# Sixteen blocks of w3 fetched in the last steps of the first network, into the tiles that later hold the product

## The chip, the cores and the metric

The kernel runs on one core of one Trainium2 chip, as one launch. The metric is the time of an execution on the device in microseconds; the time of a kernel is the median of its runs.

## The reference, cut to what matters

Three layers follow one another, all in fp32:

```
attn: state = gamma*state + k v^T; y = scale * q state      # 4 batches, 8 heads, 768 steps, head size 64
x  = attn as [3072, 512]
h  = x @ w_in [512, 2048];  g = min(max(h,1), clipped square of (h+1)/2)
x  = g @ w_out [2048, 512]                                  # first network
a  = x @ w1 [512, 1024];  b = x @ w2 [512, 1024]
h  = (a*b) @ w3 [1024, 1024]
out = h @ w_out2 [1024, 512]                                # second network
```

Nothing lies between the product with w3 and the one with w_out2, so the kernel multiplies w3 by w_out2 first (1024 x 512) and uses that product instead of both.

## The kernel before, in words

The order of the instructions is written by hand: each engine runs its own list in the order of the program, and waits only for data and for buffers. SP issues nearly all DMAs, in order; POOL issues the stores of prepared weights.

**First network.** The tokens lie in six tiles of 512. A step n multiplies one tile by one 128-wide column of w_in (`emit_h`) and adds the result of step n-1, times a row block of w_out, to the accumulators (`emit_y1`). A step holds 24 matmuls of 128 x 512. Every fp32 factor is split into a high and a low part in fp32r (`split`, L97 to L99: ScalarE copies the high part, VectorE subtracts it), and three matmuls stand for one product (`mm3`: high x high, low x high, high x low; L102 to L104). So a matmul on L102 needs the high part alone, the next one on L103 the low part.

**The last 16 steps (f = 0 to 15).** While the last tile runs, the weights of the second network, which earlier steps have converted and stored in DRAM (`spill`), come back. `fetch` issues a load on SP into one of two rings of tiles in the pool `late`: tag "f" with two buffers for blocks of w_out2 and w3, tag "y" with four buffers for blocks of w1 and w2 ("wab") and later for the first network's result. Even f: load_wo2(j - 1) splits a block of w_out2, a fetch takes the next one, and `fetch_ab(j + 1)` takes a pair of w1/w2 blocks. Odd f up to 11: `prepare_ab(j)` turns pair j into seven sums and copies (it is a Strassen-like scheme), splits them into the two stage tiles "four" and "three", and POOL stores these to DRAM (`wab_d`, 1024 and 768 KB). Before a stage tile is written again, its store has to have landed.

**The product w3 x w_out2 (u = 0 to 15).** In it a block of w3 (128 x 512, 256 KB) is split by `load_w3(u)` into one of two "ws" tiles; the split for u + 1 stands ahead of the matmuls of u, so it needs the tile that u - 1 has read. `emit_w3o(u)` is 12 matmuls into four PSUM banks. After u = 7 and u = 15 `evac_w3o` splits the four banks into tiles of tag "wc" (eight tiles of 128 x 2 x 512), which hold the product to the end. Other work is laid between: `prepare_ab(6)` at u = 0, `fetch_ab(7)` behind it, `prepare_ab(7)` at u = 3 and behind it four loads of the first network's result (`fetch_y1(0, 0)`) into the "y" buffers that the preparation frees; `add_y(0, 0)` at u = 5 adds them (VectorE, L650 to L653; the second operation, L651, needs the last of the four loads); splits (`split_y`) at u = 5 to 15; `fetch_y1(0, 1)` at u = 7 and `add_y(0, 1)` at u = 8 do the same for the other half; `load_unit` at u = 11 and 13 loads prepared weights.

**The second network** (`emit_ab`, matmuls on L673; `emit_out`, L718 to L720) follows, with TensorE nearly always busy.

Lines that the change and the prediction touch: L273 (which ring a fetch takes), L275 (the DMA of `fetch`), L559 to L563 (`load_w3`), L577 to L581 (`evac_w3o`), L842 to L858 (the fetches of the last steps), L866 to L870 (the loop over u).

Of the kernel before, what the change touches and what calls it, by code (L numbers as in the profile page):

```python
# [9 lines left out]
F32 = mybir.dt.float32  # L10
# [6 lines left out]
P = 128  # L17
# [9 lines left out]
NF1, NF2 = FF1 // P, FF2 // P  # L27
# [22 lines left out]
def retention_then_two_ffns(  # L50
# [17 lines left out]
    nc = tc.nc  # L68
# [26 lines left out]
    late = None  # L95

    def split(hi, lo, src):  # L97
        nc.scalar.copy(out=hi, in_=src)  # L98
        nc.vector.tensor_tensor(out=lo, in0=src, in1=hi, op=ALU.subtract)  # L99
# [9 lines left out]
    spill = {}  # L109
# [5 lines left out]
    def load_job(j):  # L115
        src, n, key, _ = j
        if key not in loaded:
            loaded.add(key)
            raw = cpool.tile([P, 2 * n], U32, tag="raw", name="raw")
            if key[0] == "win":  # L120

                to = raw.rearrange("p (f h a w) -> p f h a w", h=2, a=2, w=2 * P)
                of = src.bitcast(U32).rearrange("p (f a c w) -> p f a c w", a=2, c=2, w=2 * P)
                for h in range(2):
                    for c in range(2):
                        for i in range(n // 512):
                            nc.sync.dma_start(
                                out=to[64 * c:64 * c + 64, i, h], in_=of[64 * h:64 * h + 64, i, :, c]
                            )
            else:  # L130
                nc.sync.dma_start(out=raw, in_=src.bitcast(U32))
            raws[key] = raw
            ready[("raw", key)] = dma(n, max(now["dve"], now["pe"] - 4.0))

    def new_w(name):
        return wpool.tile([P, 2, 512], F32R, tag="w", name=name)
# [103 lines left out]
    def done_spill(key):  # L240
        def done(w, u):
            nc.vector.tensor_tensor(out=w, in0=w, in1=u, op=ALU.add)
            d = dram.tile([P, 512], F32, name=f"sp_{key[0]}_{key[1]}")
            nc.sync.dma_start(out=d, in_=w)
            spill[key] = d
            yield 0.73

        return done
# [16 lines left out]
    def drain_conv():  # L265
        while jobs or conv is not None:
            run_conv(1)


    arrived = {}  # L270

    def fetch(key, src):
        one = key[0] in ("wo2", "w3")  # L273
        t = late.tile([P, 512], F32, tag="f" if one else "y", name="f32", bufs=2 if one else 4)
        nc.sync.dma_start(out=t, in_=src)  # L275
        arrived[key] = t
# [221 lines left out]
    def fetch_part(i):  # L498
        y1_st[i] = []
        for m in range(NK):  # L500
            st = work.tile([P, TT], F32, tag="st", name="y1st", bufs=4)
            nc.sync.dma_start(out=st, in_=y1_part[i][m])
            y1_st[i].append(st)
# [45 lines left out]
    wo2 = {}  # L549
    w3 = {}  # L550
    wc = {}
    accs = {}

    def load_wo2(j):
        t = new_w("wo2")
        split(t[:, 0, :], t[:, 1, :], arrived.pop(("wo2", j)))
        wo2[j] = t

    def load_w3(u):  # L559
        if u < 2 * NF2:  # L560
            t = split_pool.tile([P, 2, 512], F32R, tag="ws", name="w3s")
            split(t[:, 0, :], t[:, 1, :], arrived.pop(("w3", u)))
            w3[u] = t  # L563
# [40 lines left out]
    def fetch_ab(f):  # L604
        for w in range(2):
            fetch(("wab", 2 * f + w), spill[("wab", 2 * f + w)])
# [128 lines left out]
    with tc.manual_schedule():  # L735
# [6 lines left out]
        for at_, (kind, w, f, done) in enumerate(order):  # L742
# [3 lines left out]
            for i in range(2):  # L746
                one = (w[f // 2][:, i * 512:(i + 1) * 512], 512, (kind, f + i), done(f + i))
# [28 lines left out]
        for n in range(-1, NA):  # L776
            last = n + 1 == NA
            if n < HALF - 1:
                mine = 1 if n % 2 else 2
            elif n < NF1 + 3:  # L780
                mine = 0
            elif n < NF1 + HALF - 2:
                mine = 1
            elif n < 2 * NF1 - 1:
                mine = (len(todo) - (NSTEP - 3 * TILE_PIECES) + 2 * NF1 - 2 - n) // (2 * NF1 - 1 - n)
            else:
                mine = 1 if (n + 1) % 4 < 3 else 0
            mine = [todo.popleft() for _ in range(mine) if todo]
            if n == PLAIN - 1:
                drain_conv()  # L790
                conversion.close()
                split_pool = splits.enter_context(tc.tile_pool(name="split_pool", bufs=2))
                cpool = conversion.enter_context(tc.tile_pool(name="cpool1", bufs=2))
                jobs.extend(later)
                load_job(jobs[0])
                load_job(jobs[1])
                for j in range(NF2):
                    jobs.append((w_out2[j], 512, ("wo2", j), done_spill(("wo2", j))))
                for j in range(NF2):
                    for i, w in enumerate((w1, w2)):  # L800
                        key = ("wab", 2 * j + i)
                        jobs.append((w[j], 512, key, done_spill(key)))
                for u in range(2 * NF2):
                    hf, j = divmod(u, NF2)
                    key = ("w3", u)
                    jobs.append((w3t[j][:, hf * 512:(hf + 1) * 512], 512, key, done_spill(key)))
            for i in range(2):
                if n == NF1 + (i + 1) * HALF - 4:
                    fetch_part(i)
            if n == NA - NF1:  # L810
                assert not todo
                drain_conv()
            f = n - (NA - NF1)
            if not last:
                emit_h(n + 1)
            if mine:
                piece_mm(mine[0])
                chunk_ahead(mine[0])
            if not last:
                emit_g1(n + 1)  # L820
            if mine:
                piece_ew(mine[0])
            if not last and f:
                emit_g2(n + 1)
            if n >= 0:
                emit_y1(n)
                evac_y1(n)
            if not f:

                conversion.close()  # L830
                splits.close()
                retention.close()
                split_pool = ctx.enter_context(tc.tile_pool(name="split_late", bufs=2))
                late = ctx.enter_context(tc.tile_pool(name="late", bufs=1))
                emit_g2(n + 1)
            if not last:
                emit_wo(n + 1)
            for a in mine[1:]:
                piece_mm(a)
                chunk_ahead(a)  # L840
                piece_ew(a)
            if f >= 0:  # L842
                if f % 2 and f < 2 * EARLY_AB:
                    prepare_ab(f // 2)
                elif f % 2 == 0:
                    j = f // 2
                    if j == 0:
                        fetch_ab(0)
                    else:
                        load_wo2(j - 1)  # L850
                    fetch(("wo2", j), spill[("wo2", j)])
                    if 0 <= j < EARLY_AB:
                        fetch_ab(j + 1)
                    if j == NF2 - 1:
                        fetch(("w3", 0), spill[("w3", 0)])
                elif last:
                    load_wo2(NF2 - 1)
                    fetch(("w3", 1), spill[("w3", 1)])  # L858
        pairs_psum.close()
        ps_b = ctx.enter_context(tc.tile_pool(name="ps_b", bufs=1, space=bass.MemoryType.PSUM))  # L860

# [4 lines left out]
        load_w3(0)  # L866
        for u in range(2 * NF2):
            load_w3(u + 1)
            if u + 2 < 2 * NF2:
                fetch(("w3", u + 2), spill[("w3", u + 2)])  # L870
            emit_w3o(u)
            hf, j = divmod(u, NF2)
            if j == NF2 - 1:
                evac_w3o(hf)
            if u == 0:
                prepare_ab(EARLY_AB)
                fetch_ab(EARLY_AB + 1)
            elif u == 3:
                prepare_ab(EARLY_AB + 1)
                fetch_y1(0, 0, range(4))  # L880
            elif u == 5:
                add_y(0, 0)
            elif u == 7:
                fetch_y1(0, 1, range(4))
            if u == 5:
                split_y(*ahead.pop(0))
            elif u in (6, 7, NF2):
                split_y(*ahead.pop(0))
                split_y(*ahead.pop(0))
            elif u > NF2:  # L890
                split_y(*ahead.pop(0))
            if u == NF2:
                add_y(0, 1)
            if u in (2 * NF2 - 5, 2 * NF2 - 3):
                load_unit((u - 2 * NF2 + 5) // 2)
# [104 lines left out]
```

## Time and profile before

| | |
|---|---|
| median of 3 runs | 1108.78 us (1108.28 to 1109.03) |
| the profiled execution | 1105.77 us, its span 1104.0 us |
| mean granted TensorE clock | 0.985 |
| PE busy | 1050.3 us, 95% of the span, 5444 matmuls |
| DVE, ACT, POOL busy | 698.7, 433.9, 71.5 us |
| DMA queue of SP and the like (q1) | 150.44 MB, 40.1% of 16 engines |
| DMA queue of POOL (q0) | 14.68 MB, 3.7% of 16 engines |
| chain that ended last | PE 84%, DVE 6%, DMA 5%; the loads `f<-sp_w` alone 2% |

PE is TensorE, PEld its weight loads, DVE VectorE, ACT ScalarE, SPq the instruction queue of SP. `f<-sp_w` is a load of a block of w3 from DRAM into a tile of tag "f", `f<-y_d` one of the first network's result into a tile of tag "y", `w3s` the split block, `wc` the finished product. A matmul's busy time overlaps the next one's, so the distance between two starts tells the pace, not the duration. "granted clock" 1.00 stands for 2.4 GHz and 0.50 for 1.2 GHz.

### The profile page before, as it was taken

Reading aid. Unit: us, or ns where it says so; the run is one execution under the profiler, and the core shown is the slowest. Engines: PE = TensorE matmul, PEld = TensorE weight load, DVE = VectorE, ACT = ScalarE, POOL = GpSimd, SP = SyncE. Lnnn points to the kernel's source line nnn. Section 1 sums busy time; section 2 is a strip of 40 time slices with the busy share of each in tenths; the row PEclk is TensorE's granted clock in tenths of the full one; section 3 lists DMA queues with packets and bytes.
Section 4 is the critical chain, followed back from the end, with each engine's and each line's share of the span. In section 5 each row is a group of like instructions: output and inputs, shape, how many; then the busy total and the mean of one; then the engine's idle time right before and its main releaser. Section 6 shows DMA issues by size and latency. Waiting matters only on the chain.

```text
span 1104.0 us, 14147 instructions
## 1 busy us (share of the span) xinstructions
PE 1050.3 (95%) x5444; PEld 828.7 (75%) x5444; DVE 698.7 (63%) x1130; ACT 433.9 (39%) x763; POOL 71.5 (6%) x67
## 2 busy tenths in 40 slices
PE   4789999899999999999999998689999999999998
PEld 3555578677777777777788886478888888888886
DVE  4798888688888878877835774553445334623340
ACT  1223355344444445454435664432333223412220
POOL 2212000011110100000000010000000000000000
PEclk9789999999999999999999999899999999999999
DMA  6545225254443544354303665554544345523412
GB/s 208 181 154 181 77 96 183 85 172 173 164 152 124 170 136 153 124 173 142 115 2 132 248 239 196 185 200 172 187 166 143 131 176 172 189 105 134 167 34 77
DMA packets 64116, 166.03 MB, mean 150 GB/s; under 512 B 7600, under 2 KB 15920, under 8 KB 59312
## 3 DMA queue, kind: packets, MB, share of 16 engines
q1 hardware_dynamic: 61744, 150.44, 40.1%
q0 software_dynamic: 2304, 14.68, 3.7%
q8 instruction: 43, 0.70, 0.2%
q14 instruction: 25, 0.20, 0.1%
HBM read 125.24 MB, written 39.85 MB: 150 GB/s over the span
## 4 chain that ended last, share of the span: by engine, by line
PE 84%; DVE 6%; DMA 5%; ACT 2%; SPq 1%; issue 1%; POOL 1%; ACTq 0%; POOLq 0%; DVEq 0%
PE bank_a L673 12%; PE hps L103 8%; PE y1acc L102 8%; PE hps L102 8%; PE hps L104 8%; PE y1acc L103 7%; PE y1acc L104 7%; PE bank_b L673 6%; PE oacc L718 4%; PE oacc L720 4%; PE oacc L719 4%; PE bank_c L673 3%; PE pa L372 3%; DMA f<-sp_w 2%; PE y1acc L513 2%; PE pa L348 2%
## 5 line engine op out<-in xcount | busy, mean ns | idle before, releaser
L102 PE MATMUL hps<-xh,win 128*128 128x512 f32 x384 | 154.7, 403 | 6.3 <-ACT win L98 5.0
L103 PE MATMUL hps<-xh,win 128*128 128x512 f32 x384 | 151.7, 395 | 0.5 <-DVE win L99 0.5
L104 PE MATMUL hps<-xl,win 128*128 128x512 f32 x384 | 150.8, 393 | 0.4 <-DVE xl L417 0.4
L673 PE MATMUL bank_a<-yop,unit 128*128 128x512 f32 x576 | 145.7, 389 | 0.0
L102 PE MATMUL y1acc<-gh,wo_s 128*128 128x512 f32 x340 | 139.0, 409 | 4.9 <-ACT wo_s L98 4.9
L461 ACT ACTIVATE r<-hps 128x512 f32<-128x512 f32 x96 | 57.3, 597 | 218.3 <-PE hps L104 218.3
L103 PE MATMUL y1acc<-gh,wo_s 128*128 128x512 f32 x340 | 134.2, 395 | 0.5 <-DVE wo_s L99 0.5
L104 PE MATMUL y1acc<-gl,wo_s 128*128 128x512 f32 x340 | 133.6, 393 | 0.0
L463 DVE SCALAR_TENSOR_TENSOR r<-hps,r 128x512 f32<-128x512 f32 x96 | 66.3, 691 | 101.2 <-ACT r L462 100.7
L673 PEld LDWEIGHTS bank_a<-yop,unit 128*128 128x128 f32 x576 | 108.1, 188 | 22.5
L699 DVE TENSOR_TENSOR c<-bank_b,c 128x512 f32<-128x512 f32 x24 | 16.6, 692 | 131.5 <-PE bank_b L673 131.5
L102 PEld LDWEIGHTS hps<-xh,win 128*128 128x128 f32 x384 | 72.6, 189 | 25.2 <-ACT win L98 5.7
L103 PEld LDWEIGHTS hps<-xh,win 128*128 128x128 f32 x384 | 72.6, 189 | 18.6 <-DVE win L99 1.6
L104 PEld LDWEIGHTS hps<-xl,win 128*128 128x128 f32 x384 | 72.7, 189 | 17.0 <-DVE xl L417 1.3
L102 PEld LDWEIGHTS y1acc<-gh,wo_s 128*128 128x128 f32 x340 | 64.1, 189 | 23.7 <-ACT wo_s L98 5.7
L104 PEld LDWEIGHTS y1acc<-gl,wo_s 128*128 128x128 f32 x340 | 64.1, 189 | 14.5
L103 PEld LDWEIGHTS y1acc<-gh,wo_s 128*128 128x128 f32 x340 | 64.2, 189 | 13.9 <-DVE wo_s L99 1.6
L474 ACT CAST gh<-r 128x512 fp32r<-128x512 f32 x85 | 52.9, 622 | 52.6 <-DVE r L463 52.6
L673 PE MATMUL bank_b<-yop,unit 128*128 128x512 f32 x288 | 73.1, 389 | 0.0
L475 DVE TENSOR_TENSOR gl<-r,gh 128x512 fp32r<-128x512 f32 x85 | 60.6, 713 | 14.9 <-ACT gh L474 13.8
L99 DVE TENSOR_TENSOR wo_s<-wo_f,wo_s 128x512 fp32r<-128x512 f32 x85 | 61.9, 728 | 1.9 <-ACT wo_s L98 1.9
L315 POOL TENSOR_TENSOR q_t<-q_t,decay 128x512 f32<-128x512 f32 x23 | 32.6, 1416 | 465.4 <-DMA q_t<-in_qT_dram 438.0
(152 smaller groups left out, 1716.6 us busy)
## 6 DMA issues: line engine op xcount, KB each, us to landing
unit<-wab_d SPq DMA_DIRECT2D x24, 1024.0 KB, 4.8
unit<-wab_d SPq DMA_DIRECT2D x24, 768.0 KB, 4.3
raw<-in_w_in_dram SPq DMA_DIRECT2D x64, 128.0 KB, 3.0
raw<-in_w_dram SPq DMA_DIRECT2D x16, 512.0 KB, 4.0
raw<-in_w3t_dram SPq DMA_DIRECT2D x16, 512.0 KB, 3.8
wab_d<-four POOLq DMA_DIRECT2D x8, 1024.0 KB, 5.2
raw<-in_w_out_dram SPq DMA_DIRECT2D x14, 512.0 KB, 3.6
q_t<-in_qT_dram SPq DMA_DIRECT2D x24, 256.0 KB, 4.4
```

Source lines behind the costliest of these rows:

```text
L99: nc.vector.tensor_tensor(out=lo, in0=src, in1=hi, op=ALU.subtract)
L102: nc.tensor.matmul(out=ps, lhsT=lh, rhs=rh, start=first, stop=False)
L103: nc.tensor.matmul(out=ps, lhsT=ll, rhs=rh, start=False, stop=False)
L104: nc.tensor.matmul(out=ps, lhsT=lh, rhs=rl, start=False, stop=last)
L461: nc.scalar.activation(out=r, in_=hps[n], func=AF.Relu, bias=0.5, scale=0.5)
L463: nc.vector.scalar_tensor_tensor(out=r, in0=hps.pop(n), scalar=1.0, in1=r, op0=ALU.max, op1=ALU.min)
L474: nc.scalar.copy(out=gh, in_=gs[n])
L475: nc.vector.tensor_tensor(out=gl, in0=gs[n], in1=gh, op=ALU.subtract)
L673: nc.tensor.matmul(out=ps, lhsT=x, rhs=z, start=first and kb + k == 0, stop=kb == 1 and k == 2, skip_group_check=True,)
L718: nc.tensor.matmul(out=ps, lhsT=lh, rhs=wh, start=(f == 0), stop=False)
L719: nc.tensor.matmul(out=ps, lhsT=lh, rhs=wl, start=False, stop=False)
L720: nc.tensor.matmul(out=ps, lhsT=ll, rhs=wh, start=False, stop=(f == NF2 - 1))
```

## The change

`fetch` keeps tag "f" for blocks of w_out2 alone. A new `fetch_w3(u)` takes one tile of tag "wc" and loads two blocks of w3 into its two halves. It is called once in each of the steps f = 8 to 15, at the step's end, and so all 16 blocks are issued by the end of the first network, into all eight "wc" tiles. The fetches of w3 at f = 14, at f = 15 and in the loop over u go. `load_w3` and everything else stay as they are; `evac_w3o` takes its "wc" tiles from the same eight.

```
 def fetch(key, src):
-    one = key[0] in ("wo2", "w3")
+    one = key[0] == "wo2"
     t = late.tile([P, 512], F32, tag="f" if one else "y", name="f32", bufs=2 if one else 4)
     nc.sync.dma_start(out=t, in_=src)
     arrived[key] = t
...
+def fetch_w3(u):
+
+    t = late.tile([P, 2, 512], F32, tag="wc", name="w3f", bufs=NF2)
+    for i in range(2):
+        nc.sync.dma_start(out=t[:, i, :], in_=spill[("w3", u + i)])
+        arrived[("w3", u + i)] = t[:, i, :]
...
                 fetch(("wo2", j), spill[("wo2", j)])
                 if 0 <= j < EARLY_AB:
                     fetch_ab(j + 1)
-                if j == NF2 - 1:
-                    fetch(("w3", 0), spill[("w3", 0)])
             elif last:
                 load_wo2(NF2 - 1)
-                fetch(("w3", 1), spill[("w3", 1)])
+            if f >= NF2:
+                fetch_w3(2 * (f - NF2))
...
     for u in range(2 * NF2):
         load_w3(u + 1)
-        if u + 2 < 2 * NF2:
-            fetch(("w3", u + 2), spill[("w3", u + 2)])
         emit_w3o(u)
```

## Rows read from the trace of the kernel before

**Rows 1.** Busy by stretch: PE, PEld, DVE, ACT, POOL; granted clock, DMA share, GB/s.
```profile
640.00:650.00 10.00, 10.00 (x46) 8.27 (x45) 7.47 (x17) 6.97 (x16) 1.06 (x2) 1.00 0.61 232
676.00:689.00 13.00, 12.16 (x44) 9.39 (x45) 6.48 (x16) 4.01 (x10) 1.06 (x2) 0.87 0.77 258
...
700.00:712.00 12.00, 7.07 (x17) 5.28 (x18) 6.15 (x10) 3.57 (x7) 0.00 (x0) 0.72 0.54 194
712.00:723.00 11.00, 8.11 (x34) 5.81 (x32) 9.11 (x16) 6.73 (x13) 0.00 (x0) 1.00 0.36 124
```
**Rows 2.** Waits from 676 to 741 us: total, times, longest.
```profile
ACT w3s L98 <- DMA f<-sp_w: 21.2, 4, 8.4
```
**Rows 3.** Chain that ended last, in order of time: start us, us, what.
```profile
696.48 0.32 SPq L275
696.85 7.31 DMA f<-sp_w
704.26 0.63 ACT w3s L98
...
717.66 2.62 DMA f<-y_d
```
**Rows 4.** PE in order of time: start us, us, operation; in brackets idle before, releaser.
```profile
679.47 0.63 PE L104 MATMUL w3acc<-wo,w3s 128*128 128x512 f32 x1
...
680.97 0.39 PE L102 MATMUL w3acc<-wo,w3s 128*128 128x512 f32 x1
...
704.93 0.80 PE L102 MATMUL w3acc<-wo,w3s 128*128 128x512 f32 x1 [5.04 <-ACT w3s L98]
...
721.73 0.49 PE L102 MATMUL w3acc<-wo,w3s 128*128 128x512 f32 x1 [1.85 <-ACT w3s L98]
...
723.05 0.50 PE L103 MATMUL w3acc<-wo,w3s 128*128 128x512 f32 x1 [0.83 <-DVE w3s L99]
...
725.45 0.39 PE L104 MATMUL w3acc<-wo,w3s 128*128 128x512 f32 x1
...
739.70 1.52 PE L673 MATMUL bank_a<-yop,unit 128*128 128x512 f32 x6
```
**Rows 5.** VectorE in order of time, 676 to 713 us.
```profile
676.03 0.69 DVE L99 TENSOR_TENSOR w3s<-f,w3s 128x512 fp32r<-128x512 f32 x1
...
692.55 0.42 DVE L619 TENSOR_TENSOR s<-f 128x256 f32<-128x256 f32 x1
...
696.37 0.68 DVE L99 TENSOR_TENSOR w3s<-f,w3s 128x512 fp32r<-128x512 f32 x1
...
706.12 0.68 DVE L651 TENSOR_TENSOR t__5952<-f,f 128x512 f32<-128x512 f32 x1
...
708.65 0.68 DVE L99 TENSOR_TENSOR w3s<-f,w3s 128x512 fp32r<-128x512 f32 x1
...
712.46 2.77 DVE L99 TENSOR_TENSOR wc<-w3acc,wc 128x512 fp32r<-128x512 f32 x4 [0.32 <-ACT wc L98]
```
**Rows 6.** ScalarE in order of time: a stage tile's split, a split of w3.
```profile
656.72 0.71 ACT L98 CAST three<-s 128x256 fp32r<-128x256 f32 x2
...
725.88 0.62 ACT L98 CAST w3s<-f 128x512 fp32r<-128x512 f32 x1 [2.63 <-PE w3acc L104]
```
**Rows 7.** POOL in order of time: the second store of pair 4.
```profile
648.29 0.53 POOL L627 DMA_DIRECT2D wab_d<-three  x1 [0.47 <-DVE three L99]
```
**Rows 8.** DMAs issued at 648.29, 694.80, 696.48 and 696.75 us: KB, us to landing.
```profile
wab_d<-three POOLq DMA_DIRECT2D x1, 768.0 KB, 6.9
...
f<-y_d SPq DMA_DIRECT2D x1, 256.0 KB, 2.5
...
f<-y_d SPq DMA_DIRECT2D x1, 256.0 KB, 5.0
...
wab_d<-three POOLq DMA_DIRECT2D x1, 768.0 KB, 7.2
```
**Rows 9.** SP's queue in order of time: the loads of pair 5.
```profile
635.47 2.00 SPq L275 DMA_DIRECT2D f<-sp_wab  x2
```

## Prediction

> **What bounds the kernel now.** The page gives TensorE 95% of the span, so the missing 5% are sought first. The view of busy time by stretch shows where part of them lies: in the last steps of the first network TensorE is busy without a break, but in the product w3 x w_out2 it lacks 0.84 of 13 us, 4.93 of 12 and 2.89 of 11, and in two of these stretches the granted clock is down as well, to 0.87 and 0.72 on average [rows 1]. In full-speed work that is another 13 x 0.13 = 1.7 us and 12 x 0.28 = 3.4 us. The view of waits names what ended last: ScalarE's splits of w3 wait 21.2 us in four waits for the load of their block [rows 2]. The chain shows that this is on the path: SP issues a load of the first network's result at 696.48 and the load of block 6 only behind it, which takes 7.31 us; the split follows at 704.26 and TensorE at 704.93, after 5.04 us of idling [rows 3, 4]. The second network begins at 739.70 [rows 4].
>
> **What the change does.** Sixteen loads of 256 KB stay sixteen; their place on SP and their tiles change. Eight go out at f = 8 to 11, four at f = 12 and 13, four at f = 14 and 15. No engine gets an instruction more. So the waits for w3 go; what is late next has to be worked out block by block, since ScalarE and VectorE run in order and have the preparations and the additions queued between the splits of w3.
>
> Prices: 12 matmuls at full clock take 2.72 us (0.227 each; the ten from 723.05 to 725.45, the first of which has waited, 2.40). From the start of a block's last matmul to ScalarE's split of the block two further on: 725.88 - 725.45 = 0.43 [rows 4, 6]. VectorE's part follows 0.65 behind ScalarE's, and L103 0.74 behind VectorE's (704.26 + 0.65 + 0.74 = 705.65). VectorE takes about 0.6 for a split of 512 columns (four operations in the 2.53 us from 706.12 to 708.65), and 3.82 for a preparation, from 692.55 to the next split of w3 at 696.37; 3.93 after its start it has freed the last "y" buffer, and SP issues at 696.48 [rows 3, 5].
>
> Blocks 0 to 5. The start is unchanged: block 0's split on VectorE at 676.03 [rows 5], then matmuls at 1.2 GHz (0.42 us apart at 679.47) up to block 1 at 680.97 [rows 4]. Block 1 is now split right behind block 0, at 676.63, so the preparation of pair 6 starts at 677.24 and ends at 681.06. Block 2's split needs block 0's last matmul (680.74): 681.17 on ScalarE, 681.82 on VectorE, 682.56 for L103, which is wanted at 683.9. Block 2 runs from 683.69, block 3 from 686.41, block 4 from 689.14. Block 4's split waits for block 2's last matmul: 686.19 + 0.43 + 0.65 = 687.27 on VectorE. Behind it stands preparation 7, at 687.88. Its stage tiles are free: pair 6's second store goes out 4.2 us behind its preparation's start (696.75 - 692.55 [rows 5, 8]), at 681.4, and lands by 688.6 at the 7.2 of rows 8; the tile is written again some 1.7 us into the preparation, at 689.6. Block 5 is split at 691.70 and reaches L103 at 692.44 instead of 692.09: 0.35 lost. Its last matmul starts at 694.84, block 6 runs from 695.07, block 7 from 697.79.
>
> The wait that takes the place of the old one: the last load of the result is issued at 687.88 + 3.93 = 691.81, between POOL's two stores as before, and lands 5.0 us later [rows 8], at 696.81. VectorE's second addition follows at 696.92, block 7's split 2.53 behind it [rows 5] at 699.45, L103 at 700.19 where 698.02 was possible. So 2.2 us are lost at block 7. The bounds of the 5.0 are 2.5 (a load of the same kind beside no store) and 7.31 (block 6's load) [rows 3, 8]; I take 5.0, the row of this very load at the same distance from the same stores.
>
> Blocks 8 to 15. Behind block 7's split VectorE has two splits of the result and block 8, 0.6 each, and starts the evacuation at 701.87 (the bank, ready at 701.6, is no later). From the old 712.46 there to L103 of block 10 at 723.05 [rows 4, 5] the chain is VectorE's own (evacuation, splits, then the 2.62 us of a load of the result [rows 3]), so its 10.59 us stay: 712.46. Block 10's own late load, 1.85 us of waiting at 721.73 [rows 4], lay within them and buys nothing. From that L103 to the second network it was 739.70 - 723.05 = 16.65; without the late load of block 14 it is 2.40 + 5 x 2.72 + 0.23 = 16.23. Now: 712.46 + 16.23 = 728.7.
>
> Sum: 739.7 - 728.7 = 11.0 us. It builds up so: 4.7 by preparation 7 (692.55 to 687.88), 9.9 by block 6 (704.93 to 695.07), 10.6 by the evacuation (the old half-clocked stretch lies before it), 0.4 at block 14. Behind this point TensorE sets the pace, and the second network's weights are issued earlier still, so all of it stays.
>
> What the moved loads cost. TensorE has no idle time at 640 to 650 [rows 1], so a stall of ScalarE in these steps is paid in full. Left to collide with are POOL's stores of prepared weights: pair 4's second one, issued at 648.29, takes 6.9 us and lands at 655.2 [rows 7, 8]; ScalarE writes its tile again at 656.72 [rows 6]. So it may slip 1.5 us. Where loads queued through the whole store it took 7.2 [rows 8], which is 655.5; by this nearest row the cost is nothing. The other end puts all of blocks 4 to 11 ahead of the store: 2.1 MB at the 232 GB/s of rows 1 is 9.0 us, less 1.5: 7.5 us.
> The Trainium skill (DMA: Bandwidth & Descriptors, Queues, rings and completion order) has a rule for either end. A DMA engine takes turns between the queues that have work for it, packet by packet; a longer backlog on SP then costs a store no more than a busy queue does, as the 7.2 against 6.9 suggests, and the sum stays. But a completion mark lands only after all earlier writes of that DMA engine, on any queue; the store would then be reported late by loads that started ahead of it, which is the mechanism of the second rival's dear end.
>
> **The rivals.**
> First, the result's load lands in 2.5 us. VectorE then has block 7 split at 696.95, TensorE doesn't wait there, the evacuation starts at 699.4, and 2.5 us more are won: 13.5. Against it: the stores flank the load as they did.
> Second, part is given back: the stage tile's store slips beyond its 1.5 us (up to 7.5 us lost), or the result's load takes 7.31 (2.3 lost), or the clock falls behind the waits at blocks 7 and 10 (1.7 each by the first product stretch of rows 1; after 1.85 us of waiting at 721.73 it did not fall, after 5.04 it was low [rows 1, 4]). Gain 3.5 to 9.3.
> Third, no difference: the loads would have to be off the path, and the chain through 704.26 speaks against that [rows 3].
> Fourth, slower. From the loads of pair 5 at 635.47 [rows 9] to those of pair 7, SP carries 29 transfers of 256 KB: six of pairs, three of w_out2, sixteen of w3, four stores of the first network's result. Pair 7 is due at 687.1. If they drain all along at the pace seen beside the stores, three issued between 696.48 and 704.16 [rows 3], 2.6 us each, pair 7 is there at 711, 23.8 us late, and 12.8 us are lost net. It decides from (687.1 + 11.0 - 635.5) / 29 = 2.16 us a transfer. Against it: loads overlap, each landing in 2.5 us beside no store [rows 8], and the DMA engines are 39% idle at 640 to 650 [rows 1].
>
> **How the numbers follow.** The sum stands against the profiled execution: 1105.77 - 11.0 = 1094.8. The median lies 3.0 above that execution, so I forecast 1108.78 - 11.0 = 1097.8. Chances: forecast 0.58 (its own range 1096 to 1100), first rival 0.13 (1095.3), second 0.22 (1099.5 to 1105.3), third 0.03 (1108.8), fourth 0.04 (1121.6). The range 1094.3 to 1103 leaves out the last two and the dear end of the second. A measurement of this kernel tells 0.2%, 2.2 us, from no change: faster 0.93, same 0.03, slower 0.04.
>
> **What would show it.** In the profile after: no wait of ScalarE's w3 splits for a load; loads of w3 on SP between 637 and 677; preparation 7 from near 688; waits ahead of L103 of 2.2 us at block 7 and some 3 at block 10; the first L673 near 728.7. Wrong would be: a gap on TensorE between 640 and 670, a product that starts later than it did, another landing time than 5.0 for the result's last load, a half-clocked stretch behind block 1.

## The result, and the profile after

| | before | after |
|---|---|---|
| median of 4 runs each | 1108.9 us | 1097.16 us (1096.69 to 1099.1) |
| ratio | | 0.9897, 95% interval 0.988 to 0.9914 |
| profiled execution, its span | 1105.77, 1104.0 | 1097.37, 1095.6 |
| product: first matmul with w3 to the second network's first | 675.95 to 739.70, 63.75 us | 676.53 to 731.32, 54.79 us |
| from there to the end | 364.30 us | 364.28 us |

The median fell by 11.7 us; 11.0 was forecast. The two profiled executions differ by less, 8.4 us: the product is 8.96 us shorter, its start lies 0.58 later, and what lies behind it did not change by 0.1. So in these traces all that was won was won in the product, and it was less than the forecast; the last table sets three traces of each kernel side by side. New lines push old ones down: L673 is now L680, L627 is L634, L651 is L658.

The waits from 672 to 731 us (waiter, releaser: total, times, longest):

```profile
ACT w3s L98 <- PE w3acc L104: 21.2, 9, 7.1
DVE w3s L99 <- ACT w3s L98: 13.9, 8, 4.0
...
PE w3acc L103 <- DVE w3s L99: 5.3, 5, 2.9
...
DVE t__5960 L658 <- DMA f<-y_d: 2.5, 1, 2.5
```

The row of [rows 2], ScalarE waiting for loads of w3, is gone. By chance the new first row has the same total, but its releaser is TensorE: ScalarE is ahead of the matmuls and waits for a "ws" tile to be read. VectorE now waits for a load of the result. SP's queue shows where the loads of w3 stand now (start, time up to the last issue, line, transfer):

```profile
636.05 2.00 SPq L275 DMA_DIRECT2D f<-sp_wab  x2
638.10 4.22 SPq L563 DMA_DIRECT2D w3f<-sp_w  x4
...
648.98 5.35 SPq L563 DMA_DIRECT2D w3f<-sp_w  x4
...
680.05 27.28 SPq L275 DMA_DIRECT2D f<-y_d  x8
```

Pair 5's loads start 0.58 us later than in [rows 9], and that is ahead of the first moved load: the whole trace lies 0.58 later here for another reason. Behind 680.05 there are only the eight loads of the result, no w3 between them.

TensorE (start, us, operation, idle before and releaser), to be set beside [rows 4]:

```profile
676.53 0.50 PE L102 MATMUL w3acc<-wo,w3s 128*128 128x512 f32 x1 [1.71 <-ACT w3s L98]
...
693.01 0.50 PE L103 MATMUL w3acc<-wo,w3s 128*128 128x512 f32 x1 [0.19 <-DVE w3s L99]
700.43 0.50 PE L103 MATMUL w3acc<-wo,w3s 128*128 128x512 f32 x1 [1.64 <-DVE w3s L99]
...
712.35 0.80 PE L103 MATMUL w3acc<-wo,w3s 128*128 128x512 f32 x1 [2.90 <-DVE w3s L99]
712.95 0.63 PE L104 MATMUL w3acc<-wo,w3s 128*128 128x512 f32 x1
...
731.32 1.52 PE L680 MATMUL bank_a<-yop,unit 128*128 128x512 f32 x6
```

The 5.04 us ahead of block 6 are gone. What is late next are the L103 matmuls of blocks 5, 7 and 10, each released by VectorE, as the schedule had it. VectorE's own rows, beside [rows 5]:

```profile
688.46 0.42 DVE L626 TENSOR_TENSOR s<-f 128x256 f32<-128x256 f32 x1
...
697.15 0.69 DVE L658 TENSOR_TENSOR t__5960<-f,f 128x512 f32<-128x512 f32 x1 [2.52 <-DMA f<-y_d]
...
699.69 0.68 DVE L99 TENSOR_TENSOR w3s<-w3f,w3s 128x512 fp32r<-128x512 f32 x1
...
702.10 2.47 DVE L99 TENSOR_TENSOR wc<-w3acc,wc 128x512 fp32r<-128x512 f32 x4
...
711.61 0.68 DVE L99 TENSOR_TENSOR w3s<-w3f,w3s 128x512 fp32r<-128x512 f32 x1
```

Less the 0.58, preparation 7 starts at 687.88 (forecast 687.88), the evacuation at 701.52 (701.87), and block 10's L103 at 711.77 (712.46). But then comes something that the sum had not, and that the prediction named as a sign of being wrong: a half-clocked stretch behind block 1. In the view by stretch (PE, PEld, DVE, ACT, POOL, then granted clock, DMA share, GB/s) TensorE is busy at half speed behind the wait at block 10, as the 0.63 us of the matmul at 712.95 say too:

```profile
709.00:712.00 3.00, 0.45 (x2) 0.03 (x1) 2.29 (x4) 1.14 (x2) 0.00 (x0) 0.91 0.95 382
712.00:715.00 3.00, 2.65 (x6) 2.16 (x7) 2.10 (x4) 0.00 (x0) 0.00 (x0) 0.50 1.05 435
715.00:718.00 3.00, 3.00 (x8) 2.32 (x7) 0.00 (x0) 0.55 (x2) 0.00 (x0) 0.50 0.94 393
```

From that L103 to the second network it was 18.97 us where 16.23 were worked out: 2.7 us given back.

### The profile page after: what moved, and what is told of

The parts are those of the page before. It is cut to its first block, busy times and chain, and to the rows that moved or that the text cites. A ratio compares the mean times of both kernels' runs of the same rounds, so it can differ in the third digit from the quotient of the medians.

```text
span 1095.6 us, 14128 instructions
## 1 busy us (share of the span) xinstructions
PE 1051.6 (96%) x5444; PEld 831.9 (76%) x5444; DVE 700.0 (64%) x1130; ACT 434.3 (40%) x763; POOL 72.5 (7%) x67
## 4 chain that ended last, share of the span: by engine, by line
PE 87%; DVE 7%; ACT 2%; DMA 2%; issue 1%; SPq 1%; POOL 0%; DVEq 0%; POOLq 0%; ACTq 0%
PE bank_a L680 12%; PE hps L103 8%; PE hps L104 8%; PE hps L102 8%; PE y1acc L102 8%; PE y1acc L103 7%; PE y1acc L104 7%; PE bank_b L680 6%; PE oacc L725 4%; PE oacc L726 4%; PE oacc L727 4%; PE bank_c L680 3%; PE pa L372 3%; PE y1acc L513 2%; PE pa L348 2%
## 5 line engine op out<-in xcount | busy, mean ns | idle before, releaser
L103 PE MATMUL hps<-xh,win 128*128 128x512 f32 x384 | 152.2, 396 | 0.7 <-DVE win L99 0.7
L680 PE MATMUL bank_a<-yop,unit 128*128 128x512 f32 x576 | 145.7, 389 | 0.0
L103 PE MATMUL y1acc<-gh,wo_s 128*128 128x512 f32 x340 | 134.6, 396 | 0.5 <-DVE wo_s L99 0.5
L680 PEld LDWEIGHTS bank_a<-yop,unit 128*128 128x128 f32 x576 | 108.1, 188 | 22.5
L103 PEld LDWEIGHTS hps<-xh,win 128*128 128x128 f32 x384 | 73.2, 191 | 19.0 <-DVE win L99 1.6
L103 PEld LDWEIGHTS y1acc<-gh,wo_s 128*128 128x128 f32 x340 | 64.4, 189 | 13.9 <-DVE wo_s L99 1.6
L680 PE MATMUL bank_b<-yop,unit 128*128 128x512 f32 x288 | 73.1, 389 | 0.0
L680 PEld LDWEIGHTS bank_b<-yop,unit 128*128 128x128 f32 x288 | 54.1, 188 | 11.2
```

Of the source, the lines that this page charges most:

```text
L103: nc.tensor.matmul(out=ps, lhsT=ll, rhs=rh, start=False, stop=False)
L680: nc.tensor.matmul(out=ps, lhsT=x, rhs=z, start=first and kb + k == 0, stop=kb == 1 and k == 2, skip_group_check=True,)
```

## Experiments: parts of the change

**Only blocks 0 to 5 ahead.** `if f >= NF2` becomes `if NF2 <= f < NF2 + 3`, and in the loop:

```
+            if 6 <= u + 2 < 2 * NF2:
+                fetch(("w3", u + 2), spill[("w3", u + 2)])      # tag "f", as before
```

> Blocks 0 to 5 of w3 ahead (at f = 8 to 10), blocks 6 to 15 as in the kernel before. My theory (a load of w3 costs where SP must queue it behind the loads of the result and it then flies beside the stores of pair 7): preparation 7 starts near 688.5 as after the change, but block 6's load goes out behind the result's last load at about 692 and takes 7.3 us, so TensorE waits near 5 us ahead of block 6, with the half clock behind it as before: 3 to 6 us faster than before, 5 to 8 slower than the full change. Rival (every late load costs its own wait, wherever it stands): ten of sixteen loads are still late, and the time is over 1104. Rival (only blocks 0 to 5 matter): the full gain, 1097.

1101.44 us, ratio 0.9945 (0.993 to 0.996): 6.8 us faster than before, and 4.3 slower than the change. TensorE, block 6:

```profile
700.70 0.80 PE L102 MATMUL w3acc<-wo,w3s 128*128 128x512 f32 x1 [4.88 <-ACT w3s L98]
```

The wait of [rows 4] is back at nearly its full length, 24.24 us behind the product's start instead of 28.98: the 4.7 of the sum's first part are there alone. The product took 59.21 us, 4.6 less than the 63.84 that three traces of the kernel before give in the mean (last table). So six blocks of sixteen bring 4.6 of 10.3 us by the traces, 6.8 of 11.7 by the medians. Both figures of the first theory (3 to 6 faster than before, 5 to 8 slower than the change) are missed by less than 1 us, the 1104 and the 1097 of the rivals by 2.6 and 4.4.

**Only blocks 6 and 7 ahead.** `if f >= NF2` becomes `if f == NF2 + 3`, and all other fetches of w3 stand where they did.

> Only blocks 6 and 7 ahead (at f = 11), the others as before. My theory: preparation 7 keeps its old start, 692.6, since blocks 1 and 4 are late as before; the result's last load then lands at 701.6, block 7 reaches L103 at 704.9 instead of 710.9, the evacuation starts 6.0 us earlier and that stays: 6 us faster than before, 1102 to 1104, with two blocks of sixteen. Rival (each late load costs its own): about an eighth of the gain, 1107.

1103.71 us, ratio 0.9958 (0.9943 to 0.9973): 4.5 us faster. That lies within the 1102 to 1104 that were named, and the interval, 3.0 to 6.3 us, takes in the 6 as well; the runs scatter widely (1099.98 to 1105.81), and the profiled one was the slowest. VectorE (preparation 7, the second addition) and TensorE (block 7):

```profile
696.10 0.42 DVE L626 TENSOR_TENSOR s<-f 128x256 f32<-128x256 f32 x1
...
705.02 0.69 DVE L658 TENSOR_TENSOR t__5951<-f,f 128x512 f32<-128x512 f32 x1 [3.22 <-DMA f<-y_d]
```

```profile
679.24 0.51 PE L102 MATMUL w3acc<-wo,w3s 128*128 128x512 f32 x1 [1.71 <-ACT w3s L98]
...
708.30 0.54 PE L103 MATMUL w3acc<-wo,w3s 128*128 128x512 f32 x1 [1.88 <-DVE w3s L99]
...
739.75 1.52 PE L680 MATMUL bank_a<-yop,unit 128*128 128x512 f32 x6
```

Preparation 7 keeps its old distance from the start (16.86; 16.60 before). Block 7's L103 is 29.06 us behind the start; before it was 34.99, so it comes 5.9 earlier, as expected. The product ends only 3.2 us earlier (60.51): matmuls at 1.2 GHz stand behind block 7 and again behind block 10 in this trace, where before there were none behind block 10. So two blocks of sixteen carry about a third of the gain (3.3 of 10.3 us by the traces, 4.5 of 11.7 by the medians), which no theory of equal shares gives; in the trace the size was off by the clock.

## Experiments: what is late next

**Pair 7's stores behind the result's loads.** Both stores go on SP, behind the four loads at u = 3, instead of on POOL:

```
+            if f == NF2 - 1:
+                held.append((d, t[:, 0:len(names), :].bitcast(F32)))
+                continue
             nc.gpsimd.dma_start(out=d, in_=t[:, 0:len(names), :].bitcast(F32))
...
                 fetch_y1(0, 0, range(4))
+                for to, of in held:
+                    nc.sync.dma_start(out=to, in_=of)
```

> The full change, and pair 7's two stores go out on SP behind the four loads of the result instead of on POOL. My theory (the stores beside it make the result's last load last 4.7 to 5.0 us): it lands in 2.5 to 2.7, block 7 no longer waits, 2.0 to 2.5 us faster than the change: about 1095. Rival (the load lasts that long because of where it reads or because of the load ahead of it): it still takes about 5, and the time is that of the change, 1097.

1093.16 us, ratio 0.9867 (0.985 to 0.9883). The result's last load in this kernel and in the changed one (KB, us to landing):

```profile
f<-y_d SPq DMA_DIRECT2D x1, 256.0 KB, 3.0
```

```profile
f<-y_d SPq DMA_DIRECT2D x1, 256.0 KB, 4.7
```

TensorE has no wait left at block 7, and the next is block 10:

```profile
706.89 0.50 PE L103 MATMUL w3acc<-wo,w3s 128*128 128x512 f32 x1 [0.26 <-DVE w3s L99]
712.96 0.50 PE L103 MATMUL w3acc<-wo,w3s 128*128 128x512 f32 x1 [3.05 <-DVE w3s L99]
```

The stores did stretch the load, though it still took 3.0 where 2.5 to 2.7 were expected. From the product's start at 678.64 to L103 of block 10 it is 34.32 us, in the change's trace 35.82: 1.5 us won, where 2.0 to 2.5 were expected. The product took 52.17 us, 2.6 less than in the change's trace; the rest of that is the clock, with 7 matmuls at 1.2 GHz behind block 10 here and 12 there. The medians differ by 4.0, but they are of different series of runs, and the intervals of the two ratios overlap.

**Two of the result's loads in the idle f buffers.**

```
-        one = key[0] == "wo2"
+        one = key[0] == "wo2" or key in (("y", 0, 0, 2), ("y", 0, 0, 3))
```

> The full change, and two of the four loads of the result's first half go into the two f buffers that the change leaves idle, instead of into pair 7's buffers. My theory (what is late next are the two waits of VectorE's additions for a load whose buffer comes free late): the first half is there before it is wanted, no wait at block 7; the second half finds its buffers free by 695, so the wait of 2.9 us at block 10 shrinks to about 1.4 (VectorE's own work), and the half-clocked stretch of some 3 us behind it goes. 3.5 us faster than the change from the waits alone, up to 6 with the clock: 1091 to 1094. Rival (the waits are VectorE's own work, and the loads are hidden behind it): within 1 us of the change, 1097.

1091.91 us, ratio 0.986 (0.9845 to 0.9874). The product took 48.53 us. TensorE, and the clock behind block 10:

```profile
709.74 0.50 PE L103 MATMUL w3acc<-wo,w3s 128*128 128x512 f32 x1 [1.33 <-DVE w3s L99]
```

```profile
709.00:712.00 3.00, 2.27 (x10) 1.89 (x11) 2.49 (x5) 0.36 (x1) 0.00 (x0) 1.00 0.51 211
712.00:715.00 3.00, 3.00 (x15) 2.49 (x14) 1.30 (x2) 1.14 (x2) 0.00 (x0) 1.00 0.00 0
```

The wait at block 7 is gone, the one at block 10 is 1.33 us, and the clock stays at 1.00 behind it. So the two waits were for a buffer that came free late, and the half clock was a part of their price.

**The second additions a block later** (from u = 8 to u = 9, on top of the last kernel):

```
-            if u == NF2:
-                add_y(0, 1)
...
+            elif u == NF2 + 1:
+                add_y(0, 1)
```

> The version with the result's loads in the idle f buffers, and the second half's additions one block later on VectorE (u = 9 instead of u = 8), so that block 10's split no longer stands behind them. My theory (the 1.33 us that block 10 still waits are VectorE's own queue): block 10 doesn't wait, block 11 waits 0 to 0.3, 1.0 to 1.6 us faster than that version: 1090.5. Rival (the wait moves on to block 11 whole): 1092, no difference.

1090.15 us over 5 runs, ratio 0.9837 (0.9824 to 0.9849): the lowest of all, 7.0 us below the changed kernel, though its interval overlaps that of the version above by a little. No wait at block 10 or 11 is left in its trace, as the theory had it. The product ran from 680.04 to 725.55, 45.51 us, 3.0 less than in the version above; of these the wait of 1.33 is the edit's, and the rest is the clock, since the start of the product ran at full clock this time and 8 matmuls at 1.2 GHz stood there in the version above.

## Experiments: did the moved loads cost anything

**All sixteen at f = 12 to 15, four a step.** `if f >= NF1 - 4`, with two calls of `fetch_w3`.

> All sixteen blocks ahead, but four a step at f = 12 to 15 instead of two a step at f = 8 to 15, so that no w3 load flies beside the stores of pairs 3 and 4. My theory (the moved loads cost TensorE nothing where the change put them): the time of the change, 1097 within 1 us; the store of pair 4 lands about 7 us after its issue again instead of 8.3. Rival (part of the gain was lost to that company): faster than the change by more than 1 us. Rival (the place matters because the late blocks come late): slower by more than 1 us.

1097.87 us, ratio 0.9897 (0.9882 to 0.9913), the change's ratio to the fourth digit. Pair 4's second store, issued at 650.85, landed in 6.6 us. The first moved loads go out at 654.28, so they still met its second half; the theory's "about 7" holds.

**Twice the transfers.** Behind each load in `fetch_w3`:

```
+            copy = dram.tile([P, 512], F32, name=f"copy{u + i}")
+            nc.sync.dma_start(out=copy, in_=spill[("w3", u + i)])
```

> The full change, and behind each load of w3 a copy of the same block from DRAM to DRAM, so that SP carries twice the transfers at f = 8 to 15. With the change pair 4's second store lands 0.13 us before ScalarE writes its tile again, so this store is what a heavier load should delay first. If DMA engines take turns between SP's queue and POOL's, the store lands little later than 8.3 us and TensorE loses 0 to 2 us ahead of 676. If the store waits for all that was put on SP before it ended (some 1 to 2 MB more at 350 GB/s, 3 to 6 us), TensorE gets a gap of 2.5 to 6 us near 658 and one of 1 to 4 near 647, and the time is 1100 to 1107.

1098.33 us, ratio 0.9905 (0.9891 to 0.9919), not to be told from the change's. Pair 4's second store (POOL's issue, landing) and ScalarE's next write of its tile, in the changed kernel:

```profile
648.88 0.53 POOL L634 DMA_DIRECT2D wab_d<-three  x1 [0.47 <-DVE three L99]
```

```profile
wab_d<-three POOLq DMA_DIRECT2D x1, 768.0 KB, 8.3
```

```profile
657.31 0.71 ACT L98 CAST three<-s 128x256 fp32r<-128x256 f32 x2
```

and with the copies, issued at 651.41:

```profile
wab_d<-three POOLq DMA_DIRECT2D x1, 768.0 KB, 8.6
```

```profile
660.02 0.71 ACT L98 CAST three<-s 128x256 fp32r<-128x256 f32 x2
```

648.88 + 8.3 = 657.18, 0.13 us ahead of the write: the change used up nearly all of the 1.5 us. With the copies, 651.41 + 8.6 = 660.01, and ScalarE writes at 660.02, some 0.2 us late by the pattern of the steps; TensorE shows no gap from 600 to 671 in either. So this place is at its edge.

But beside this store the load was not doubled. SP's issues became slow, and the copies took the places of loads (start, time up to the last issue, line, transfer; the changed kernel, then the one with the copies):

```profile
654.43 0.95 SPq L275 DMA_DIRECT2D f<-sp_wo  x1
655.42 2.37 SPq L563 DMA_DIRECT2D w3f<-sp_w  x4
```

```profile
651.51 1.17 SPq L563 DMA_DIRECT2D w3f<-sp_w  x1
652.73 1.27 SPq L565 DMA_DIRECT2D copy<-sp_w  x1
...
659.20 0.47 SPq L565 DMA_DIRECT2D copy<-sp_w  x1
```

Up to the landing SP put out eight transfers of 256 KB in either kernel: the four at 648.98, one at 654.43 and three of the four from 655.42 on there, four loads and four copies here. So the 0.3 us between 8.3 and 8.6 are not the price of twice the load. Pair 5's second store tells more, with three transfers issued beside it in the changed kernel and nine with the copies:

```profile
wab_d<-three POOLq DMA_DIRECT2D x1, 768.0 KB, 7.3
```

```profile
wab_d<-three POOLq DMA_DIRECT2D x1, 768.0 KB, 9.9
```

There the longer backlog cost the store 2.6 us, which nothing waited for. The dear end of the second rival did not come in any run, but this experiment does not show that it could not have come at pair 4's store under a heavier load.

## Experiments: each kernel once or twice more

> The kernel before once more, for a second trace. In the profiled execution the product's matmuls began at 675.95 and took 63.75 us up to the second network; its time, 1105.77, lies 3 us under the median. My theory: the product takes within 1.5 us of 63.75 again (the clock's phase can move 1.7 us), and what differs between executions lies ahead of it, a start anywhere from 676 to 680. Rival: the product itself takes some 3 us more in a usual execution, and the profiled one was a lucky one in the stage that the change touches.

> As before_2, a third trace of the kernel before: the same two expectations.

> The changed kernel once more. In its first trace the product took 54.79 us, with 3 us of half clock behind the wait at block 10. My theory: that wait is 2.9 us again, and the clock falls behind it again or not, so 51.8 to 55; the start lies anywhere from 676 to 680. Rival: the first network's last steps suffer from the moved loads in some executions; then a gap on TensorE shows at 640 to 668.

> As after_2, a third trace of the changed kernel: the same two expectations.

| trace | product from | to | us |
|---|---|---|---|
| before | 675.95 | 739.70 | 63.75 |
| before_2 | 676.69 | 740.56 | 63.87 |
| before_3 | 679.30 | 743.20 | 63.90 |
| after | 676.53 | 731.32 | 54.79 |
| after_2 | 678.80 | 730.85 | 52.05 |
| after_3 | 679.25 | 732.94 | 53.69 |

Before, the product is the same within 0.2 us; after, it varies by 2.7, and the clock is in that: half clock at the product's start in two of the three (not in after_2), and behind block 10 in all. The start varies by 3.4 us before and by 2.7 after. So the profiled execution of before was 3 us fast ahead of the product, not in it, and no gap on TensorE shows at 640 to 668. What varies lies ahead of the moved loads: from pair 5's loads to the product's start it is 40.44 to 40.49 us in all six traces (675.95 - 635.47 and 676.53 - 636.05 are both 40.48), so the moved loads cost TensorE nothing there. Mean to mean the product lost 63.84 - 53.51 = 10.3 us; the timed 11.7 has an interval of 9.5 to 13.3.

## Why the prediction was right

- **The wait removed.** As forecast: no split of w3 waits for a load, and the two partial versions put 4.7 us at the start of preparation 7 and 5.9 at block 7, the two places named. The change gave w3 an earlier place on SP and more tiles at once; no run gives it more tiles at its old place, so what each brings alone is not shown.
- **The wait that took its place.** As forecast, the result's last load, whose buffer pair 7 frees late. Its 5.0 us were 4.7. With the stores out of its way it took 3.0 and block 7 did not wait, so the first rival's mechanism was right and its condition was not met; its price of 2.5 us was 1.5 in the trace up to block 10.
- **Blocks 8 to 15.** VectorE's own chain nearly kept its length: 10.59 us from the evacuation to L103 of block 10, 10.25 now (702.10 to 712.35). The 16.23 behind it were mis-sized: 18.97, 17.76 and 17.82 in the three traces. I put the second fall of the clock, 1.7 us, into the second rival because a wait of 1.85 us had not brought it; the new wait, of which the prediction itself said "some 3", is 2.9 in one piece, and behind it the clock fell in all three traces and in three versions that keep it (late_burst, doubled and stores_behind). It stayed up behind 1.33, and behind the 1.64 to 1.71 at block 7 of the same traces. That is the one term that was wrong, by 1.5 to 2.7 us.
- **The contention.** The cost was nothing, as taken, but a landing of 7.2 was 8.3: the nearest row had three loads queued, here there were eight, and from 648.9 to 657.2 the DMA engines were busy all along (share 1.01, 354 GB/s). By the Trainium skill's rule of turns (DMA: Bandwidth & Descriptors, Queues, rings and completion order) a DMA engine changes between the queues that have work for it, packet by packet. The prediction concluded from it that a longer backlog costs a store no more than a busy queue does. That step did not hold: 6.9 became 8.3, and at pair 5's store 7.3 became 9.9 with six more transfers. Whether turns or the order of completion marks set these times, the runs don't tell.
- **The slower rival.** Pair 7's loads went out at 676.82 and landed within 4 us; the 29 transfers were issued within 42 us and landed within some 45, not 75.
- **The median.** 1097.8 forecast, 1097.16 measured. That it came so close is in part luck. In the profiled pair the clock took 2.7 us back and the shorter chain with the earlier evacuation gave only 0.7, so the product lost 8.96 us and not 11.0; over three traces of each kernel it lost 10.3. That lies within the interval of the timed gain; what makes the medians differ by 11.7 besides is not shown, but the start of the product varies by some 3 us between executions, ahead of the moved loads.

## What to carry to other kernels

Here the costliest load was late because another stood ahead of it in an in-order queue; asking which two or three loads stand behind a blocked one says more than counting loads. Before a wait is removed, work out what the in-order engines have queued next: here the same buffers, freed late, cost another 5 us that one changed line removed. Price a new wait of some 3 us on TensorE with the half-clocked stretch behind it.

## What the runs showed of the hardware

SP's issues themselves took longer beside POOL's stores: two loads of 256 KB went out within 0.94 us at 675.84 with no store of POOL's under way, four took 4.22 us at 638.10 and 5.35 at 648.98 just behind stores, and 2.37 at 655.42; the cause is not shown. And a wait of 2.9 to 3.05 us in one piece was followed by half clock, at once or within 1.4 us, in six traces of six, while waits of 1.9 and 0.8 us with one matmul between them were not in three traces of the kernel before, and were in the two partial versions. A single wait of 1.88 us, at block 7 with only blocks 6 and 7 ahead, was followed by it too.
